# Another order of all 1610 words in a linear-attention and gated-MLP kernel's list

## The chip, the cores and the metric

The kernel runs on one core of a Trainium2 chip. The time is device microseconds of one execution; the comparisons rest on the median of several runs. The engines are PE (TensorE: matmuls, with PEld for loading weights), DVE (VectorE), ACT (ScalarE), POOL (GpSimd) and SP (SyncE), whose queue issues nearly all transfers.

## The reference

Gated linear attention with a state per head, then a gated MLP on its output, all in fp32:

```python
# q, k, v, alpha: (batch 4, heads 8, seq 768, head_dim 48)
for t in range(S):
    state = alpha[:, :, t, :, None] * state + einsum('bhd,bhe->bhde', k[:, :, t], v[:, :, t])
    y[:, :, t] = einsum('bhd,bhde->bhe', q[:, :, t], state)
x = y.transpose(0, 2, 1, 3).reshape(B * S, H * D)     # 3072 tokens x 384
g = x @ w_gate                                        # 384 x 1536
out = (g * sigmoid(g) * (x @ w_val)) @ w_out          # 1536 x 384
```

## The kernel before

The attention is cut into 16 units of 192 positions (four per batch), all 8 heads at once; a unit has three chunks of 64. The MLP is cut into 8 blocks of 384 tokens (two units each) times 12 slices of 128 of the inner width: 96 steps. Blocks 0 and 1 are done in two halves: steps 0 to 6 are the first seven slices of block 0, steps 7 to 13 those of block 1, 14 to 18 and 19 to 23 the rest; then come twelve steps for each further block. So g7 is the first product that needs block 1, that is, units 2 and 3, and g84 the first that needs block 7, units 14 and 15.

The weights come as 64-bit words. Each of the 20 groups of weights (two slices, the first three of one) is loaded raw, cut to fp32 in three steps, and split into a high part and a low part in fp32r. Products are the sum of three: high by high, high by low, low by high. So a g, a v and an o are nine matmuls of 384 columns each (three row blocks by three products).

All instructions are written down by one list, ORDER: 1610 words, each of the form engine:name@banks. The engine is t (PE), v (DVE), s (ACT), g (POOL) or y (SP); digits behind @ name the PSUM banks. The program goes through the list and writes each word's instructions to its engine's queue. Every engine works through its own queue in order, and waits at an instruction for whatever its operands need. There is no other scheduler. The words that matter here (u is a unit, c a chunk, n a group of weights, s a step):

- Lau, Lku, Lqu, Vu.i: loads of alpha, keys, queries, values. For units 0 to 3, pau, pku, pqu widen them (L405) and Tau, Tku, Tqu turn them on PE (L417), eau, eku, cqu copy them out; later units are transposed on DVE (tru, tku, tqu, L397).
- Gu, fu: the two scans of the decay on DVE (L461, L470); qu, mku: queries and keys scaled; qcu, vcu: copies of a part of the queries (L492) and of the values into U (L498).
- Su: scores (L552). mau.i: masked scores from PSUM to X on DVE (L586). Ku.c, kcu.c: keys turned on PE and copied out on ACT (L515, L516); kru.i is the same on DVE (L527).
- Buc or Bwu: the carry into the next chunks (L576); adu.c adds or copies it into the values or into SE (L599, L606, L608); deu carries SE into the next unit (L614).
- Yu: the unit's outputs (L630, L631, L647); yhu.i, ylu.i: their high and low part (L661 on ACT, L665 on DVE).
- Ru.kt, xu.kt: for units 0 and 1 the rows are brought into xT by PE; for all others xru.kt moves them from X to xT by transfers on SP (L701): ten for each unit. One xT serves a block.
- wln, wnv0 to wnv2, wna, wnp: load of a weight group (L298, L301), its cutting steps (L160, L161, L164), its high part (L341), its low part (L345).
- gs, sls, vs, hs, hhs, hls, os: gate product, SiLU (L724), value product (L716), h = SiLU times value (L728), its high part (L732) and low part (L737), output product (L748). g has one PSUM bank, called gps (bank 6), v one, called vps (bank 5): the next g waits for the SiLU of the one before, the next v for its h.
- otu.i, osu.i, plu.i: output rows copied, stored, and loaded again; wri, wci, Lcu, cku: loads and tests of the value ranges.

A transfer on SP waits for the one issued eight before it, besides what its operands need.

Of the kernel before, what the change touches and what calls it, by code (L numbers as in the profile page):

```python
# [48 lines left out]
y:La3 y:V1.1 y:V1.0 y:V1.3 y:V1.5 y:V1.2 v:de1 g:vc1 v:yl0.0 v:yl0.1 v:w3v2 s:pa2 t:S1@30 t:Bw1@2 s:qc1 s:pa3 v:ma1.0
v:ma1.1 y:wl4 s:w4v0 v:w4v1 s:ad1.0 v:ma1.2 v:w4v2 g:w4a g:w4p t:Ta2@65 s:ea2 v:G2 s:ad1.2 t:Y1@41 s:yh1.0 v:yl1.0  # L50
t:R0.1@6 t:R0.0@7 v:x0.0 s:x0.1 t:Ta3@35 t:R0.2@6 y:Lq2 s:pq2 t:Tq2@04 y:V2.4 y:V2.0 y:Lk2 s:pk2 y:V2.1 t:Tk2@27
s:yh1.1 v:yl1.1 t:R1.2@1 s:cq2 s:x0.2 s:x1.2 t:R1.0@0 s:x1.0 t:R1.1@4 s:x1.1 v:mk2 t:K2.0@7 y:wl10 t:K2.2@2 s:kc2.2
y:wl5 s:w5v0 t:g0 s:kc2.0 t:K2.1@1 s:kc2.1 y:V2.3 y:V3.3 y:V2.5 y:Lk3 g:pk3 t:Tk3@04 v:f2 v:q2 s:ea3 y:Lq3 s:pq3
g:lm0 g:qc2 s:sl0 s:w3a g:w3p y:V2.2 v:de2 s:vc2 t:S2@27 t:Bw2@1 s:ad2.0 s:ad2.2 t:g1 s:sl1 v:w5v1 t:v0 v:G3 v:f3
v:ma2.2 v:h0 v:ma2.0 y:wl6 t:Tq3@13 s:cq3 g:q3 v:w5v2 y:wl12 y:V3.1 v:mk3 s:hh0 y:V3.2 y:V3.0 v:ma2.1 y:V3.4 t:g2
g:qc3 g:lm1 s:w6v0 v:w6v1 y:wl8 s:w8v0 t:v1 v:h1 y:wl16 y:V3.5 v:de3 t:K3.0@1 s:kc3.0 s:w5a s:hh1 g:hl1 v:w6v2
t:S3@70 v:ma3.1 v:ma3.2 v:w5p y:wl9 y:wl7 t:K3.1@2 s:kc3.1 t:Y2@43 y:V4.5 s:yh2.0 v:yl2.0 s:yh2.1 v:yl2.1 v:ma3.0
y:wl11 y:V4.3 y:V4.0 y:La4 s:w6a g:w6p y:wl14 y:xr2.0 y:xr2.1 y:Lk4 y:xr2.2 t:Bw3@2 t:v2 s:sl2 v:h2 t:g3 t:v3 v:hl0
t:o0 t:o1 s:w9v0 v:w9v1 v:w9v2 s:vc3 s:w7v0 v:w7v1 s:ad3.0 v:w8v1 v:w7v2 s:w7a v:w8v2 v:w7p s:hh2 s:sl3 v:h3 g:hl2
s:w8a v:w8p t:K3.2@2 s:w9a v:w9p t:Y3@01 s:hh3 t:g4 s:yh3.0 s:yh3.1 v:yl3.1 v:yl3.0 y:xr3.2 y:V5.4 s:w11v0 v:w11v1  # L60
v:w11v2 s:sl4 t:v4 v:h4 s:w10v0 v:w10v1 v:w10v2 t:o2 g:hl3 s:w12v0 v:w12v1 s:hh4 v:hl4 s:kc3.2 s:w10a v:w10p v:tr4
t:o3 t:g5 s:sl5 t:v5 v:h5 s:w11a g:w11p v:w12v2 t:o4 y:wl13 s:w13v0 v:G4 s:hh5 g:hl5 t:g6 s:sl6 t:v6 v:h6 s:hh6 g:hl6
y:xr3.0 y:xr3.1 t:g7 s:sl7 t:v7 v:tk4 v:mk4 t:g8 y:V5.1 y:Lq4 y:V5.3 v:tq4 y:V5.5 y:V4.4 s:w12a y:V4.1 y:V5.2 t:o5
# [1038 lines left out]
```

## Time and profile before

| | us |
|---|---|
| median of 3 runs | 559.82 (559.21 to 559.98) |
| the profiled execution's own time | 563.47 |
| span of its trace | 561.8 |
| PE busy | 537.3 (96%) |
| DVE busy | 378.5 (67%) |
| ACT busy | 253.7 (45%) |
| POOL busy | 165.3 (29%) |

The span is the time from the first to the last instruction of the profiled execution; its own time holds 1.7 us more around it. The durations below are of that execution. Busy shares are averages over the whole span; a single place is read from the waits, the chain and the timelines.

### The profile page before, as it was taken

What the parts mean: (1) busy time and instruction counts of PE and PEld (TensorE: products, weight loads), DVE (VectorE), ACT (ScalarE), POOL (GpSimd) and SP (SyncE); (2) the same over time, 40 slices, a digit from 0 to 9 for tenths busy, and PEclk for the clock granted to TensorE, in tenths of its full rate; (3) what the DMA queues carried; (4) which work ended last, traced back from release to release, by engine and by line L of the source; (5) the groups of instructions that cost most, each with busy time, mean ns of one, the idle gap of its engine ahead of it and who ended that gap; (6) DMA issues with size and microseconds to landing.
All of it is one profiled execution on the core that took longest, in us unless ns stands there. A gap on an engine that the chain in (4) does not pass through costs nothing.

```text
span 561.8 us, 13698 instructions
## 1 busy us (share of the span) xinstructions
PE 537.3 (96%) x5510; PEld 524.7 (93%) x5510; DVE 378.5 (67%) x605; ACT 253.7 (45%) x570; POOL 165.3 (29%) x164
## 2 busy tenths in 40 slices
...
GB/s 254 198 224 312 193 158 127 220 132 68 126 161 132 139 125 179 195 118 85 146 159 86 163 66 155 170 32 125 109 145 29 72 80 119 98 123 119 148 121 115
...
## 3 DMA queue, kind: packets, MB, share of 16 engines
...
q8 instruction: 44, 0.72, 0.6%
...
## 4 chain that ended last, share of the span: by engine, by line
PE 88%; DVE 3%; DMA 3%; issue 1%; ACT 1%; SPq 1%; POOL 0%; DVEq 0%; ACTq 0%; POOLq 0%
PE g L716 26%; PE v L716 26%; PE ops L748 25%; PE A L576 3%; PE y L647 2%; PE s L552 2%; DMA xT<-X 1%; DMA raw<-in_moe_w_val_dram 1%; PE y L630 1%; PE y L631 1%; SPq L701 1%; DVE AT L470 1%; DMA Le<-in_alpha_dram 1%; DVE Gs L461 1%; DVE t L161 1%
## 5 line engine op out<-in xcount | busy, mean ns | idle before, releaser
L716 PE MATMUL g<-xT,w 128*128 128x384 f32 x864 | 167.9, 338 | 5.2 <-ACT h L724 3.5
L716 PE MATMUL v<-xT,w 128*128 128x384 f32 x864 | 167.6, 338 | 0.0
L748 PE MATMUL ops<-w,hh 128*128 128x384 f32 x576 | 157.5, 335 | 0.0
L716 PEld LDWEIGHTS g<-xT,w 128*128 128x128 f32 x864 | 150.8, 188 | 6.9 <-ACT h L724 3.8
L737 POOL TENSOR_TENSOR hl<-h,hh 128x384 fp32r<-128x384 f32 x65 | 69.4, 1069 | 297.8 <-ACT hh L732 277.3
L716 PEld LDWEIGHTS v<-xT,w 128*128 128x128 f32 x864 | 152.3, 189 | 0.4
L728 DVE TENSOR_TENSOR h<-h,v 128x384 f32<-128x384 f32 x96 | 53.1, 553 | 115.4 <-PE v L716 91.4
L748 PEld LDWEIGHTS ops<-w,hh 128*128 128x128 f32 x576 | 105.3, 188 | 0.9 <-DVE part L756 0.8
L732 ACT CAST hh<-h 128x384 fp32r<-128x384 f32 x96 | 49.1, 512 | 124.6 <-DVE h L728 90.0
L748 PE MATMUL ops<-w,hl 128*128 128x384 f32 x288 | 96.8, 336 | 0.0
L724 ACT ACTIVATE h<-g 128x384 f32<-128x384 f32 x96 | 46.9, 489 | 97.0 <-PE g L716 88.5
L527 DVE STREAM_TRANSPOSE K<-Gs 32x384 f32<-32x384 f32 x96 | 54.7, 570 | 2.4 <-PE A L576 0.5
L748 PEld LDWEIGHTS ops<-w,hl 128*128 128x128 f32 x288 | 54.0, 188 | 0.1
L486 POOL TENSOR_TENSOR X<-trq,AT 112x768 f32<-112x768 f32 x13 | 22.7, 1746 | 34.3 <-DMA xT<-X 10.4
L737 DVE TENSOR_TENSOR hl<-h,hh 128x384 fp32r<-128x384 f32 x31 | 17.5, 565 | 21.0 <-ACT hh L732 19.5
L345 POOL TENSOR_TENSOR w<-t,w 128x768 fp32r<-128x768 f32 (+1 forms) x14 | 25.5, 1825 | 19.8 <-ACT w L341 18.5
L470 DVE TENSOR_TENSOR_SCAN AT<-AT,back 128x771 f32<-128x771 f32 x16 | 30.4, 1899 | 0.6
L586 DVE TENSOR_TENSOR X<-s,mask 64x384 f32<-64x384 f32 (+1 forms) x48 | 26.4, 552 | 5.0 <-PE s L552 4.0
L461 DVE TENSOR_TENSOR_SCAN Gs<-AT,inj 128x772 f32<-128x772 f32 x16 | 28.0, 1752 | 0.6 <-ACT AT L794 0.5
L661 ACT CAST X<-y 112x384 fp32r<-112x384 f32 x28 | 12.3, 482 | 26.8 <-PE y L647 23.1
L318 ACT ACTIVATE wc<-wc,wbias 128x384 f32<-128x384 f32 x36 | 23.3, 647 | 1.2
L576 PE MATMUL A<-V,K 64*48 64x48 f32 (+1 forms) x720 | 22.1, 207 | 1.0 <-issue 0.9
...
## 6 DMA issues: line engine op xcount, KB each, us to landing
xT<-X SPq DMA_DIRECT2D x84, 72.0 KB, 2.2
...
```

Of the source, the lines that this page charges most:

```text
L345: eng.tensor_tensor(out=lo, in0=src, in1=hi.bitcast(F32), op=ALU.subtract)
L461: nc.vector.tensor_tensor_scan(*(x.rearrange("p g t -> p (g t)")[:, ::-1] for x in (Gs, AT, inj)), 0.0, op0=ALU.mult, op1=ALU.add)
L470: nc.vector.tensor_tensor_scan(Af, Af, back[:, 1 : n + 1], back[:, 0:1], op0=ALU.mult, op1=ALU.add)
L527: nc.vector.transpose(out=bass.AP(k0.tensor, k0.offset, [k0.ap[0], (G * 2 * D, NU), (2 * D, G), (1, 32)]), in_=Kg[j * BO + x : j * BO + x ...
L576: nc.tensor.matmul(to[j * BO : j * BO + D, g - gs.start, :], Ks[r, x, g, KC[j]], Vd[r, x, g, VC[j]], start=(x == 0 or not whole), stop=(x ...
L586: nc.vector.tensor_tensor(out=X[r, z, f * GF : (f + 1) * GF, :].rearrange("r g (c t) -> r g c t", c=NU), in0=sps[f][r].rearrange("r g (c t ...
L716: nc.tensor.matmul(pt, wsp[kind, f][a][:, kt * P : (kt + 1) * P], xT[blk][:, b_, kt, :], start=(n == 0), stop=(n == 3 * KT - 1),)
L724: nc.scalar.activation(h, acc.pop(("g", blk, f)), AF.Silu)
L728: nc.vector.tensor_tensor(out=h, in0=h, in1=acc.pop(("v", blk, f)), op=ALU.mult)
L732: nc.scalar.copy(out=hh, in_=acc["h", blk, f])
L737: eng.tensor_tensor(out=hl, in0=acc.pop(("h", blk, f)), in1=hh.bitcast(F32), op=ALU.subtract)
L748: nc.tensor.matmul(ops[blk][i], h[b_][:, i * P : (i + 1) * P], wsp["o", f][a], start=(first and n == 0), stop=(last and n == 2),)
```

## The change

Only the text of ORDER changes: the same 1610 words in another order. 84 of them go to another engine. The words of each engine are now 366 for PE (as before), 451 for DVE (443), 396 for ACT (387), 106 for POOL (123) and 291 for SP (as before). Most words of PE and DVE name other banks or stand at other places. The functions are untouched.

```diff
 ORDER = """
-y:La0 s:pa0 t:Ta0@23 s:ea0 y:wl0 v:w0v0 v:w0v1 y:Lk0 v:w0v2 g:w0a y:La1 s:pa1 g:w0p t:Ta1@53 y:Lq0 s:pq0 t:Tq0@71
+y:La0 y:wl0 s:pa0 t:Ta0@20 s:ea0 y:La1 s:pa1 y:Lq0 s:pq0 y:Lk1 y:Lk0 t:Ta1@67 s:pk0 v:w0v0 v:w0v1 v:w0v2 s:w0a g:w0p
...
```

Three places follow. First ACT (Activation) in unit 0, where the carried state SE, the values' copy U and the keys K are copied; before:

ACT before, from the last cutting step of w2 on:

```order
L160 ACTIVATE t2_353<-raw2_351,lbias_120 128x384
L606 COPY SE_109<-s0_0_240 48x96 x2
L606 COPY SE_109<-A2_0_296 48x96 x2
L515 COPY K0_105<-kps1_1_367 64x4x48
L516 COPY K0_105<-kps1_1_367 64x4x48
L599 COPY V0_77<-A2_0_296 48x8x48 x2
L515 COPY K0_105<-kps1_0_377 64x4x48
L516 COPY K0_105<-kps1_0_377 64x4x48
L515 COPY K0_105<-kps1_2_356 64x4x48
L516 COPY K0_105<-kps1_2_356 64x4x48
L341 CAST w1_386<-t1_199 128x384
```

The same place on ACT now:

```order
L794 COPY trq1_290<-pt1_2_1_286 128x128x3
L606 COPY SE_109<-s0_0_234 48x96 x2
L606 COPY SE_109<-A2_0_295 48x96 x2
L599 COPY V0_77<-A2_0_295 48x8x48 x2
L160 ACTIVATE t2_352<-raw2_350,lbias_120 128x384
L498 COPY U_101<-V0_77 64x3x96 x2
L515 COPY K0_105<-kps1_2_357 64x4x48
L516 COPY K0_105<-kps1_2_357 64x4x48
L515 COPY K0_105<-kps1_1_370 64x4x48
L516 COPY K0_105<-kps1_1_370 64x4x48
```

The copies of SE and of the state stand together and first; the copy of U, which POOL did, has come in behind them, and the cast of w1 has gone to POOL. In the whole list the masked scores of unit 0 (ma0.0 to ma0.2) stood ahead of the copies of SE (ad0.2) and now stand behind them.

Second, ACT around g7: raw13 is the load of weight group 13, h0_6 the SiLU of step 6 and h1_0 that of step 7. ACT before:

```order
L724 ACTIVATE h0_5_1279<-g0_5_1269 128x384
L341 CAST w11_1292<-t11_1215 128x768
L160 ACTIVATE t13_1308<-raw13_1305,lbias_120 128x768
L732 CAST hh0_5_1312<-h0_5_1279 128x384
L724 ACTIVATE h0_6_1326<-g0_6_1316 128x384
L732 CAST hh0_6_1339<-h0_6_1326 128x384
L724 ACTIVATE h1_0_1360<-g1_0_1350 128x384
```

ACT now:

```order
L732 CAST hh0_5_1302<-h0_5_1270 128x384
L341 CAST w11_1307<-t11_1256 128x768
L341 CAST w12_1310<-t12_1299 128x768
L724 ACTIVATE h0_6_1335<-g0_6_1315 128x384
L732 CAST hh0_6_1338<-h0_6_1335 128x384
L724 ACTIVATE h1_0_1370<-g1_0_1360 128x384
L515 COPY K0_105<-kps3_2_1138 64x4x48
L516 COPY K0_105<-kps3_2_1138 64x4x48
L160 ACTIVATE t13_1374<-raw13_1047,lbias_120 128x768
```

The first step of weight group 13 stood ahead of the SiLU of step 6 and stands behind that of step 7.

Third, SP at the end of the moves from X to xT for block 1 (X0 holds unit 2, X1 unit 3), SP before:

```order
L701 DMA xT1_1026<-X0_103 48x2x192 x2
L701 DMA xT1_1026<-X1_104 32x2x192
L701 DMA xT1_1026<-X1_104 48x2x192 x2
L435 DMA V1_78<-in_v_dram 64x4x48
L301 DMA raw13_1305<-in_moe_w_gate_dram 128x3x256
L301 DMA raw13_1305<-in_moe_w_val_dram 128x3x256
L701 DMA xT1_1026<-X1_104 48x2x192 x2
L701 DMA xT1_1026<-X1_104 32x2x192
L701 DMA xT1_1026<-X1_104 16x2x192
L701 DMA xT1_1026<-X1_104 48x2x192 x2
L701 DMA xT1_1026<-X1_104 16x2x192
```

SP now:

```order
L298 DMA raw14_1134<-in_moe_w_out_dram 128x768
L301 DMA raw14_1134<-in_moe_w_gate_dram 128x3x256
L701 DMA xT1_1039<-X1_104 16x2x192
L701 DMA xT1_1039<-X1_104 48x2x192 x2
L701 DMA xT1_1039<-X1_104 16x2x192
L701 DMA xT1_1039<-X1_104 48x2x192 x2
L701 DMA xT1_1039<-X1_104 32x2x192 x2
L701 DMA xT1_1039<-X1_104 48x2x192 x2
L701 DMA xT1_1039<-X0_103 32x2x192
L701 DMA xT1_1039<-X0_103 48x2x192 x2
L301 DMA raw16_1243<-in_moe_w_gate_dram 128x3x256
```

The loads among the moves of unit 3 have gone ahead of them (raw13 stands further up), and the last three moves of unit 2 have come behind them.

## Rows read from the trace of the kernel before

**Rows 1.** The page's first lines: span, busy time and share of each engine.

```profile
span 561.8 us, 13698 instructions
PE 537.3 (96%) x5510; PEld 524.7 (93%) x5510; DVE 378.5 (67%) x605; ACT 253.7 (45%) x570; POOL 165.3 (29%) x164
```

**Rows 2.** PE's waits over the span: waiter, releaser, us in total, times, longest.

```profile
PE g L716 <- ACT h L724: 3.5, 1, 3.5
PE y L647 <- POOL U L498: 2.7, 1, 2.7
```

**Rows 3.** The chain that ended last, in order of time: start us, us, what.

```profile
33.32 0.90 PE y L647 x32
...
47.25 1.56 PE v L716 x9
...
63.47 7.51 DMA xT<-X
...
77.21 5.97 DMA raw<-in_moe_w_val_dram
...
85.11 2.00 PE g L716 x9
87.11 2.88 PE v L716 x9
89.99 1.67 PE g L716 x9
...
215.02 1.34 issue
```

**Rows 4.** PE's timeline, 0 to 92 us: start us, us, engine, line, operation, tiles, count.

```profile
18.10 0.72 PE L576 MATMUL A<-V,K 128*48 128x48 f32 x24
...
24.91 0.90 PE L552 MATMUL s<-X,Gs 48*64 48x64 f32 x48
...
39.47 1.83 PE L716 MATMUL g<-xT,w 128*128 128x384 f32 x9
...
79.90 1.73 PE L716 MATMUL v<-xT,w 128*128 128x384 f32 x9
```

**Rows 5.** Two stretches: length, busy us and count per engine, PEclk, DMA share, GB/s.

```profile
30.00:35.00 5.00, 2.29 (x65) 1.96 (x61) 3.35 (x5) 2.15 (x8) 4.80 (x4) 1.00 0.82 275
...
87.00:88.00 1.00, 1.00 (x5) 1.00 (x4) 0.96 (x2) 0.80 (x2) 0.29 (x1) 0.50 0.83 151
```

**Rows 6.** ACT's timeline, 21 to 46 us; in brackets idle before and releaser.

```profile
21.03 0.48 ACT L606 COPY SE<-s 48x96 f32<-48x96 f32 x2 [2.25 <-DVE X L586]
...
22.05 0.31 ACT L515 COPY K<-kps 64x192 f32<-64x192 f32 x1
...
45.15 0.89 ACT L498 COPY U<-V 64x288 f32<-64x288 f32 x2
```

**Rows 7.** POOL's timeline, 29 to 41 us.

```profile
29.13 4.14 POOL L498 COPY U<-V 64x288 f32<-64x288 f32 x2
...
38.84 2.00 POOL L405 COPY wide<-L 128x576 f32<-128x576 f32 x1 [2.76 <-ACT xT L691]
```

**Rows 8.** DVE's timeline at the masks of unit 0 and the low parts of unit 3.

```profile
19.23 1.71 DVE L586 TENSOR_TENSOR X<-s,mask 128x384 f32<-128x384 f32 x3
...
69.08 1.02 DVE L665 TENSOR_TENSOR X<-y,X 112x384 fp32r<-112x384 f32 x2
```

**Rows 9.** Groups by line and shape, DVE and POOL: busy us, mean ns, idle before.

```profile
L737 DVE TENSOR_TENSOR hl<-h,hh 128x384 fp32r<-128x384 f32 x31 | 17.5, 565 | 21.0 <-ACT hh L732 19.5 <-issue 1.5
L345 DVE TENSOR_TENSOR w<-t,w 128x768 fp32r<-128x768 f32 x6 | 5.7, 955 | 0.2 <-ACT w L341 0.2
L486 DVE TENSOR_TENSOR X<-trq,AT 112x768 f32<-112x768 f32 x2 | 2.2, 1090 | 0.0
...
L345 POOL TENSOR_TENSOR w<-t,w 128x768 fp32r<-128x768 f32 x10 | 20.1, 2016 | 15.4 <-ACT w L341 14.2 <-POOL V L438 0.9
```

**Rows 10.** The page's part 6, DMA issues: count, KB each, median us to landing.

```profile
xT<-X SPq DMA_DIRECT2D x84, 72.0 KB, 2.2
```

**Rows 11.** SP's timeline, the last seven moves for block 1.

```profile
78.37 4.48 SPq L701 DMA_DIRECT2D xT<-X  x7
```

More of the change, by code (lines that the diff above doesn't have):

```diff
@@ L49 @@
[L49 to L63, printed above, removed]
@@ L129 @@
-s:hh77 y:os71.0 y:Lc10 v:ad15.0 v:ad15.1 y:Lc0 s:ck0 y:os71.2 t:g78 t:v78 t:o76 y:wr12 y:xr14.1 v:ma15.2 s:sl78 v:h78
-s:hh78 v:hl78 y:Lc5 s:ck5 t:g79 s:sl79 g:hl77 t:o77 t:o78 t:v79 v:h79 s:vc15 t:Y15@10 s:yh15.0 s:yh15.1 s:hh79 t:g80
-v:yl15.0 v:yl15.1 y:xr15.1 s:sl80 y:wr20 y:xr15.2 y:xr14.2 t:v80 s:wc12 v:h80 t:g81 v:hl79 t:v81 s:sl81 t:g82 t:o79
-s:hh80 v:hl80 t:o80 s:ck10 s:sl82 v:h81 t:v82 s:wc20 v:h82 t:g83 t:v83 s:hh81 g:hl81 t:o81 s:hh82 g:hl82 t:o82 s:sl83
-v:h83 s:hh83 v:hl83 t:o83 y:wr1 y:wr14 y:wr23 y:xr15.0 t:g84 s:wc14 v:ot83.0 y:os83.0 s:sl84 s:wc23 t:v84 v:h84
@@ L139 @@
[L139 to L141 removed]
+y:La0 y:wl0 s:pa0 t:Ta0@20 s:ea0 y:La1 s:pa1 y:Lq0 s:pq0 y:Lk1 y:Lk0 t:Ta1@67 s:pk0 v:w0v0 v:w0v1 v:w0v2 s:w0a g:w0p
+v:G0 t:Tq0@35 s:pk1 v:f0 v:q0 t:Tk0@12 v:mk0 y:wl1 s:w1v0 y:Lq1 v:w1v1 y:wl3 y:V0.3 s:ea1 v:G1 y:V0.1 y:V0.0 y:V0.2
@@ new lines @@
+t:Tk1@43 s:ek1 t:K0.1@5 s:kc0.1 t:S0@60 t:K0.0@3 s:kc0.0 v:w1v2 t:K0.2@1 s:kc0.2 s:w3v0 v:mk1 v:f1 g:pq1 t:Tq1@72
+s:cq1 y:V0.5 y:V0.4 t:Bw0@5 s:ad0.2 s:ad0.0 y:wl2 s:w2v0 y:V1.3 g:qc0 v:ma0.0 t:K1.2@4 y:wl4 s:vc0 y:V1.0 s:kc1.2
+t:K1.1@2 s:kc1.1 y:V1.4 y:V1.1 t:K1.0@3 s:kc1.0 v:ma0.1 v:ma0.2 t:Y0@70 y:V1.2 s:yh0.0 s:yh0.1 v:w3v1 v:w2v1 y:La2
+s:pa2 y:V1.5 g:w1a v:w1p s:w4v0 y:La3 s:pa3 g:q1 v:de1 t:S1@62 t:Bw1@3 s:ad1.0 v:w2v2 g:w2a y:Lq2 v:w3v2 v:yl0.0
+v:yl0.1 t:R0.1@7 g:qc1 v:ma1.0 v:ma1.1 v:w4v1 v:ma1.2 t:Ta2@05 s:ea2 v:G2 s:ad1.2 g:vc1 t:Y1@41 s:yh1.0 v:yl1.0
@@ new lines @@
+t:K3.1@4 s:kc3.1 y:wl9 v:f3 v:q3 t:S3@16 s:w6v0 t:K3.0@3 s:kc3.0 g:qc2 v:ma2.0 v:ma2.1 t:Y2@42 s:yh2.0 y:V3.4 y:wl8
+v:w5v2 s:w5a v:de3 t:Bw3@0 s:ad3.0 s:yh2.1 v:h1 s:hh1 v:w6v1 v:w6v2 v:yl2.0 v:ma3.2 g:qc3 v:ma3.0 v:yl2.1 y:wl12
+y:wl11 y:xr2.0 y:Lk4 y:wl13 y:xr2.1 s:w6a v:w6p t:v2 v:h2 v:ma3.1 t:o0 g:w5p t:g3 t:v3 v:w7v1 s:w9v0 s:hh2 v:hl2
+g:hl1 t:o1 t:o2 v:w7v2 s:w8v0 s:vc3 y:wl14 v:w8v1 t:K3.2@1 v:w9v1 v:w8v2 s:sl3 v:h3 s:w7a v:w7p v:w9v2 s:w8a v:w8p
+s:w10v0 v:w10v1 s:w9a v:w9p t:Y3@20 s:yh3.0 t:g4 s:sl4 s:hh3 g:hl3 s:yh3.1 v:yl3.1 t:v4 v:h4 v:yl3.0 y:xr3.1 y:xr3.0
@@ new lines @@
+y:xr3.2 y:xr2.2 y:wl16 t:g5 s:w11v0 v:w11v1 v:w10v2 t:v5 s:sl5 v:h5 s:hh4 v:hl4 v:w11v2 s:w10a v:w10p t:o3 t:o4
+s:w12v0 v:w12v1 s:hh5 v:hl5 v:w12v2 s:w11a v:w11p s:w12a g:w12p v:tk4 t:g6 t:v6 s:sl6 v:h6 s:hh6 g:hl6 v:tr4 v:G4
+y:V5.2 y:Lq4 y:V4.2 t:o5 t:g7 s:sl7 s:kc3.2 s:w13v0 t:v7 v:h7 t:o6 s:ot6.1 y:V4.4 y:os6.1 s:ot6.0 y:os6.0 y:La5 v:mk4
+v:w13v1 v:f4 s:w14v0 s:hh7 g:hl7 y:wl15 y:V5.0 y:V4.1 y:V4.0 y:wl17 t:g8 s:sl8 t:v8 v:h8 s:hh8 g:hl8 v:w14v1 t:g9
+s:w16v0 v:tq4 s:ot6.2 s:sl9 t:v9 v:h9 v:w13v2 t:o7 v:w14v2 s:w14a g:w14p v:q4 v:tr5 t:g10 t:v10 s:sl10 y:V5.4 s:w13a
@@ new lines @@
+s:sl16 s:ot13.2 s:hh15 g:hl15 v:w17v2 s:w17a g:w17p v:w18v2 s:w18a g:w18p t:v16 v:h16 v:ad4.2 y:La6 v:tr6 t:g17 t:v17
+s:sl17 v:h17 t:o14 t:o15 y:V5.1 y:Lk6 v:tk6 v:kr5.2 s:hh17 g:hl17 v:kr5.3 t:Y4@56 s:yh4.0 s:yh4.1 v:yl4.0 v:yl4.1
+y:V5.3 y:V5.5 v:G6 v:mk6 t:S5@10 t:B5@2 v:kr6.2 v:kr6.1 t:g18 s:sl18 t:v18 t:g19 s:hh16 g:hl16 t:o16 t:o17 y:Lq6
+y:os13.1 y:wl19 s:w19v0 v:w19v1 v:w19v2 s:w19a y:V6.0 y:os13.2 v:h18 v:f6 s:qc5 v:ma5.0 y:V6.4 y:V6.2 v:kr6.3 g:w19p
+s:sl19 t:v19 v:h19 y:V6.1 y:wr8 y:V6.5 y:pl18.2 s:hh18 g:hl18 v:tq6 s:hh19 g:hl19 t:g20 s:wc8 s:sl20 s:vc5 t:o18
@@ new lines @@
+v:h35 g:qc9 g:hl33 t:o33 t:o34 s:hh35 v:hl35 v:G10 v:f10 t:o35 v:ot35.2 s:ot35.1 y:os35.1 t:g36 t:v36 s:wc3 s:wc19
+v:ad8.1 v:ad8.2 t:Y8@41 s:sl36 v:h36 y:V9.0 y:V10.0 s:hh36 g:hl36 y:V9.4 y:wr15 y:V9.1 y:V10.1 v:ot35.0 y:Lq10
+v:kr9.3 s:yh8.0 s:yh8.1 v:yl8.0 v:kr9.2 t:g37 s:sl37 t:v37 v:h37 g:mk10 t:g38 s:sl38 t:v38 v:h38 v:yl8.1 t:g39 t:o36
+s:hh37 g:hl37 t:o37 t:v39 s:hh38 v:hl38 s:sl39 v:h39 s:hh39 g:hl39 t:g40 s:sl40 t:v40 y:V9.5 v:de9 s:vc9 y:V10.4
+t:g41 y:V10.2 y:xr8.0 y:xr8.2 y:xr8.1 v:tq10 g:q10 v:h40 s:sl41 v:kr9.1 t:S9@01 t:B9@2 s:qc10 v:tr11 t:o38 t:o39
@@ new lines @@
+v:ad10.2 s:sl46 t:v46 y:V11.1 v:h46 s:hh46 v:kr11.0 t:g47 s:sl47 y:os35.2 t:o45 g:hl46 t:o46 s:vc10 t:Y10@60 y:V11.2
+y:xr9.0 v:q11 v:tr12 t:S11@15 v:kr11.2 v:ma11.2 y:V11.3 y:V11.0 t:B11@2 s:yh10.0 s:yh10.1 v:yl10.0 y:Lk12 v:tk12
+y:wr7 t:v47 v:h47 v:de11 v:G12 g:mk12 s:hh47 v:hl47 t:g48 s:sl48 t:v48 v:h48 s:hh48 y:wr4 s:wc7 y:Lq12 y:V12.5
+y:os35.0 y:V12.2 g:hl48 t:g49 s:sl49 t:o47 s:ot47.0 y:La13 v:yl10.1 y:xr10.0 v:ot47.1 v:ad11.0 y:os47.1 y:wr11 s:wc26
+t:v49 v:h49 s:hh49 g:hl49 v:ad11.1 t:g50 t:v50 s:sl50 v:h50 s:ot47.2 t:g51 y:V12.1 t:o48 t:v51 s:sl51 v:h51 t:g52
@@ new lines @@
+t:o49 s:hh50 g:hl50 t:o50 v:tq12 s:hh51 g:hl51 v:f12 y:os47.0 y:xr10.2 y:xr10.1 y:wr9 s:wc11 t:v52 s:sl52 v:h52
+s:hh52 v:kr12.0 s:wc4 g:hl52 g:qc11 t:g53 s:sl53 t:v53 v:h53 v:q12 v:ma11.1 y:V12.3 y:V12.4 t:g54 y:Lk13 v:tr13
+y:Lq13 y:wr0 t:v54 s:sl54 v:h54 v:tk13 t:g55 t:o51 t:v55 t:o52 g:vc11 v:ma11.0 t:Y11@01 y:V13.2 v:kr12.3 v:G13 v:mk13
+s:hh54 y:wr28 v:kr12.2 g:hl54 s:sl55 v:h55 s:hh53 v:tq13 s:wc9 s:yh11.0 s:yh11.1 v:yl11.0 v:kr12.1 y:V12.0 y:V13.3
+v:yl11.1 y:os47.2 y:wr2 t:g56 g:hl53 t:o53 t:o54 s:sl56 s:hh55 s:wc0 g:hl55 y:La14 t:v56 v:h56 s:hh56 v:hl56 y:xr11.2
@@ new lines @@
+y:xr11.0 t:g57 s:sl57 v:f13 t:v57 s:qc12 t:S12@12 t:B12@0 s:ad12.0 y:xr11.1 g:q13 v:h57 v:ma12.1 v:kr13.3 v:ma12.0
+t:o55 t:o56 t:g58 y:V13.0 y:V13.5 s:hh57 g:hl57 y:wr5 y:Lk14 y:V13.1 v:kr13.0 v:ad12.1 v:ad12.2 v:ma12.2 t:v58 s:sl58
+v:h58 s:hh58 t:g59 t:o57 v:tr14 y:Lq14 v:kr13.1 g:hl58 v:G14 s:sl59 t:v59 v:h59 s:hh59 g:hl59 t:o58 v:tk14 y:La15
+g:mk14 v:f14 t:g60 t:v60 s:sl60 v:h60 s:hh60 t:g61 s:sl61 y:V13.4 t:v61 t:o59 v:hl60 v:h61 s:hh61 g:vc12 t:Y12@65
+y:V14.3 s:ot59.0 y:os59.0 g:vc13 s:wc5 s:yh12.0 s:wc2 s:yh12.1 v:kr13.2 v:yl12.0 v:de13 t:S13@12 t:B13@0 v:ad13.0
@@ new lines @@
+v:yl12.1 v:ad13.1 s:qc13 v:ad13.2 s:ot59.1 s:ot59.2 t:g62 s:sl62 s:wc28 t:o60 t:v62 v:h62 s:hh62 g:hl62 v:kr14.0
+t:g63 s:sl63 v:ma13.2 v:ma13.0 t:v63 v:h63 v:tq14 t:g64 t:v64 g:hl61 t:o61 t:o62 y:wr21 y:V14.4 y:V14.0 y:Lc5
+v:ma13.1 s:ck5 v:kr14.1 s:sl64 v:h64 t:Y13@51 y:V14.5 y:xr12.0 y:xr12.2 y:os59.2 y:os59.1 y:xr12.1 y:wr32 v:q14
+v:kr14.2 v:kr14.3 s:yh13.0 s:yh13.1 s:hh63 y:V14.1 y:V14.2 y:Lk15 s:hh64 g:hl63 t:S14@26 t:B14@0 v:ma14.2 v:yl13.0
+v:de14 v:ad14.0 v:tk15 t:g65 t:v65 t:o63 s:sl65 v:h65 s:hh65 g:hl65 s:wc32 t:g66 s:sl66 v:tr15 y:Lq15 v:yl13.1 t:v66
```

128 lines of the change are left out of this document (51 added, 77 removed).

## The prediction

> **What bounds the kernel now.** Read the share of busy time first, then TensorE's waits, then the chain of waits in order of time, then the engines' timelines at the places that the chain names. The profiled execution spans 561.8 us, and TensorE is busy for 537.3 of them [rows 1]. A word g, v or o of the MLP is nine matmuls and 1.56 us [rows 3]; there are 288 of them, 449 us, and no order makes them fewer. From 85.11 us until the last output product the chain of waits is TensorE and nothing else, but for five short pauses in which it waited for nothing that the profile shows, the longest 1.34 us [rows 3]. So an order can win in the first 85 us only, and can lose anywhere.
>
> In these 85 us the reader is to see two losses. The first is the way to the first product g0, which starts at 39.47 [rows 4]: the scores of unit 1 start at 24.91 [rows 4], the outputs of unit 1 wait 2.7 us for U on GpSimd [rows 2] and end at 34.22 [rows 3]. The second stands at g7, the first product of block 1. The product before it, v6, ends at 79.90 + 1.73 = 81.63 [rows 4]; g7 starts at 85.11 after 3.5 us of waiting for a SiLU [rows 2, 3], and then runs 2.00 us, v7 2.88 and g8 1.67 in place of 1.56 each [rows 3]. That is 1.87 us more, in a stretch where the granted clock is 0.50, the lower of TensorE's two levels [rows 5]. The place costs 3.48 + 1.87 = 5.35 us. Between g0 and g7 nothing is lost: 42.16 us passed, and the words there, counted at their durations in the chain, come to about 42.
>
> **The change part by part.** Every word stays; only places move, and 84 of the 1610 words change their engine.
>
> Unit 0. Before, ScalarE copies the first carried state (SE) at 21.03, after 2.25 us of idling for a mask product on VectorE [rows 6], which comes ahead of it in the old list. In the new list the copies stand ahead of the mask products, so they wait for TensorE's carry alone. The carry ended at 18.82 [rows 4] and nothing ahead of it is moved back, so the copies run at about 18.6 to 20.5. The mask products keep their place behind VectorE's chain of scans (19.23 to 20.9, rows 8), which I find unchanged: its inputs come as early as before. The copy of U for unit 0 goes from GpSimd to ScalarE (0.89 us, rows 6) and ends near 22.1, so Y0 ends near 22.9 instead of 24.9: 2.0 us won. ScalarE's six key copies of unit 1 (0.31 each, rows 6) follow to 24.0; S1 and its carry need the banks that these empty, and take about 2.5 us: 26.6.
>
> Unit 1. The copy of U on GpSimd took 4.14 us, of which the chain charges 2.7 to TensorE [rows 2, 7]. In the new list a cast of w2 and a copy of q, about 1 us each, stand ahead of it on GpSimd, behind VectorE's last step of w2 near 24.2; I put it at 26.0 to 30.1, with the slow duration of 4.14. Y1 can start when ScalarE has copied unit 1's state, near 28.3, and then ends near 31.0, for 34.22 before. Behind it the way to g0 was 39.47 - 34.22 = 5.25 us. It holds the repacking matmuls, two transposes and ScalarE's copies. A widening goes from ScalarE to GpSimd (2.00 us there, rows 7), and one copy from VectorE to ScalarE, so I give it 5.3 to 5.6. g0 starts near 36.3: 3.2 us won. The bounds are 0, if GpSimd and the copies take back what unit 0 gave, and 4.5, if U is copied in 0.9 us as on ScalarE.
>
> Weigh the slow copy once more: GpSimd's 4.14 us against 0.89 us for the same two copies on ScalarE [rows 6, 7]. The Trainium skill ("SBUF — State Buffer", section "Who interferes with whom") says that a VectorE instruction with two inputs from SBUF contends with a GpSimd instruction that reads SBUF, and that one of them is blocked outright. This speaks against the change, which gives VectorE more such subtractions beside GpSimd's copies. By the rule the copy stays at about 4 us, as I have taken it; without it the sum would be some 2 us lower.
>
> g7. Before, ScalarE's list has the first step of weight group 13 (raw13) ahead of the SiLU of step 6, and that load was issued at 77.21 and took 5.97 us [rows 3]. In the new list the load is issued ahead of unit 2's second move into xT, and its step stands behind the SiLU of g7. So the wait of 3.48 us goes, and with it the 1.87 us at the low clock: 5.35 us.
>
> What is late next at g7 is xT itself. It needs 20 moves from X to xT on the sync queue. The last group waits for VectorE's subtraction yl3.0; it ended at 70.10 before [rows 8]. In the new list 13 moves stand behind it with nothing between. Seven took 4.48 us to issue, 0.64 each [rows 11], and a move lands in 2.2 us [rows 10]: 13 x 0.64 + 2.2 = 10.5 us. VectorE's work from the scan of unit 1 to yl3.0 grows: the low parts of w1, w3, w4 and w6 come over from GpSimd (about 0.55 + 3 x 0.955), with one hl (0.565) and q3 (1.09); h4 (about 0.55) and a step of w10 (about 0.96) now stand ahead; one hl, one copy and the low part of w5 go (2.1). That is 4.5 us more [rows 9]. Of the old 50.9 us from 19.23 to 70.10, by the same counting, 43 were work and 8 were waits for TensorE. If the earlier TensorE work takes half of those waits away, yl3.0 ends near 70.9 and xT is complete near 81.4; if none goes, 74.6 and 85.1.
>
> TensorE itself is ready for g7 at 36.3 + 42.2 + 1.56, since the new list has o5 ahead of g7: 80.1. So the new wait is 1.3 us at best and 5.0 at worst. I take 2.1, nearer the best, since the same earlier start that frees VectorE's waits is what moves g0. Such a wait is shorter than the 2.71 us of unit 1, across which the granted clock stayed at 1.00 [rows 2, 5], so I add nothing for the clock.
>
> Later. Y4 and Y12 now use the banks of g and v, so the next g waits for their evacuation: S and B cover 1.8 us of the two casts and two subtractions, about 2.1. I add 0.6 for both together and for tight places that I don't see; bounds 0 and 3. VectorE's work between two h that are six steps apart, counted as above, exceeds TensorE's by 0.4 us at most, so I see no place where it must be late.
>
> Sum: -3.2 - 5.35 + 2.1 + 0.6 = -5.85 us. On the profiled execution's own time, 563.47, that gives 557.6; the median of the runs shown is 559.82, 3.65 lower, and there it gives 554.0.
>
> **The rivals.** *VectorE becomes the bound of the first 85 us.* For it: the 4.5 us more work, and low parts of weights on VectorE just ahead of the g and v that need them (that of w7 is due within 0.2 us of g4 by my count). Against it: the same subtraction takes 0.955 us there and 2.016 on GpSimd [rows 9], so the products get their weights sooner. All 8 us of waits stay, and xT is complete at 85.1; with 1.87 us at the low clock again, and one o more done than before, the gain is 1.56 + (85.11 - 85.1), about 1.6, and the time 558.2.
>
> *The order hardly does what it says:* what g0 wins is waited for again by loads. For it: the chip's transfers set the old stalls, one move took 7.51 us to land [rows 3] where 2.2 is usual [rows 10], and a list cannot shorten them. Against it: at g7 the load that was waited for is issued some 15 us earlier. Then g0 stays at 39.5, xT comes at 85 and the time is within 1 us of 559.8.
>
> *Slower, by the last block.* Before, 13 words (20.3 us) stand between the end of Y15 and g84; now 8 (12.5 us). On the sync queue 19 issues end with the moves for g84, two groups of unit 14 and a load among them. If those 19 start only when the last subtraction of unit 15 is done, 2.6 us after Y15 (two casts, two subtractions and an h, about 0.5 each), the last is issued 12.2 us later (0.64 each); at 7.51 us to land, as behind bulk loads [rows 3], g84 waits 2.6 + 12.2 + 7.5 - 12.5 = 9.8 us, and 1.87 more at the low clock. With -5.85 this gives +5.8, 565.6. It decides from 5.85 us on, that is, when the queue is held and the moves land late together. Against it: unit 14's moves need nothing of unit 15, and with them issued before, 10 x 0.64 + 2.2 + 2.6 = 11.2 us fit in 12.5. The Trainium skill ("DMA: Bandwidth & Descriptors", section "Queues, rings and completion order") has each DMA engine consume a queue's descriptors in ring order. The 7.51 us agree with that. By that rule the price stands wherever bulk is in front, and the chance hangs on the order alone.
>
> **How the numbers follow.** The forecast, 554.0, has 0.60; its own range is 551.5 to 556.5. VectorE as the bound has 0.17, no change 0.08, the last block or a like stall 0.12, and a gain beyond the forecast's range 0.03. The low end, 551.3, is -3.2 - 5.35 with no new wait, 8.55 below the median. The high end, 559.5, takes in the second case and stops short of no change; about 0.17 lies above it and 0.03 below. A difference of 0.2%, 1.1 us, is about what a measurement of this kernel can tell from none. Faster by more holds all of the forecast, the gain beyond it and nearly all of the second case: 0.79. Within: the third case, less its tails: 0.07. Slower: 0.14.
>
> **What would show it.** In the new trace: ScalarE's SE copies start before 19 us and wait for TensorE; Y1 ends near 31; g0 starts near 36.3; no SiLU wait at g7, but a wait there for a move into xT, under 3 us, and a granted clock of 1.00 through it; from g7 to the end a chain of TensorE alone. I am wrong if g0 starts after 38.5, if the clock falls to 0.50 at any place after 40 us, or if TensorE waits more than 2 us anywhere after g8.

## The result, and the profile after

The kernel after took 553.57 us, the median of 4 runs (552.74 to 554.53); the kernel before took 559.52 beside it (558.24 to 559.98). The ratio is 0.987, with a 95% interval of 0.983 to 0.991. The forecast was 554.0.

The page's first lines of the profiled execution (552.74 us), then TensorE's waits (waiter, releaser, us in total, times, longest), against [rows 1, 2]:

```profile
span 551.0 us, 13702 instructions
PE 536.4 (97%) x5510; PEld 523.7 (95%) x5510; DVE 384.8 (70%) x612; ACT 258.7 (47%) x581; POOL 136.5 (25%) x146
```

```profile
PE pt L417 <- POOL sel L369: 5.1, 1, 5.1
PE pt L417 <- ACT wide L405: 1.5, 2, 1.3
PE g L716 <- issue: 1.0, 1, 1.0
...
PE v L716 <- DVE h L728: 0.3, 1, 0.3
```

The two rows that I read in the kernel before, 3.5 us for a SiLU and 2.7 for U [rows 2], are both gone. What is left is the start (pt) and crumbs. Next TensorE's timeline at S1 and g0, ScalarE's at unit 0, and GpSimd's at unit 1 (start us, us, engine, line, operation, tiles, count; idle before in brackets):

```profile
23.20 0.92 PE L552 MATMUL s<-X,Gs 48*64 48x64 f32 x44 [0.29 <-ACT K L516]
...
34.47 1.85 PE L716 MATMUL g<-xT,w 128*128 128x384 f32 x9
```

```profile
18.24 0.50 ACT L606 COPY SE<-s 48x96 f32<-48x96 f32 x2
...
20.95 0.89 ACT L498 COPY U<-V 64x288 f32<-64x288 f32 x2
```

```profile
25.59 0.91 POOL L498 COPY U<-V 64x288 f32<-64x288 f32 x2
```

g0 starts at 34.47, for 39.47 [rows 4]. The copy of U that took 4.14 us [rows 7] takes 0.91. At g7 the chain of waits (start us, us, what), VectorE's yl3.1 and yl3.0, the sync queue's moves, and the clock (the number before the last two) are:

```profile
76.90 1.57 PE ops L748 x9
78.47 1.58 PE g L716 x9
80.05 1.56 PE v L716 x9
...
203.39 1.01 issue
```

```profile
67.26 0.56 DVE L665 TENSOR_TENSOR X<-y,X 112x384 fp32r<-112x384 f32 x1 [0.49 <-ACT X L661]
...
68.19 0.55 DVE L665 TENSOR_TENSOR X<-y,X 112x384 fp32r<-112x384 f32 x1
```

```profile
67.84 8.86 SPq L701 DMA_DIRECT2D xT<-X  x13
```

```profile
75.00:80.00 5.00, 5.00 (x30) 5.00 (x30) 5.00 (x5) 1.74 (x3) 2.70 (x2) 1.00 0.59 166
```

TensorE goes through o5, g7 and v7 without a gap, 1.56 to 1.58 us each, where before stood 3.48 us of waiting and a clock of 0.50 [rows 3, 5].

One thing did not fit. The two spans differ by 10.8 us, the medians by 5.95. The profiled run of before (563.47) lay above all its timed runs. So which of its two losses belongs to every run? The experiments ask that.

### The profile page after: what moved, and what is told of

It reads as the page before. It is cut to its first block, busy times and chain, and to the rows that moved or that the text cites. A ratio compares the mean times of both kernels' runs of the same rounds, so it can differ in the third digit from the quotient of the medians.

```text
span 551.0 us, 13702 instructions
## 1 busy us (share of the span) xinstructions
PE 536.4 (97%) x5510; PEld 523.7 (95%) x5510; DVE 384.8 (70%) x612; ACT 258.7 (47%) x581; POOL 136.5 (25%) x146
## 4 chain that ended last, share of the span: by engine, by line
PE 90%; DVE 3%; SPq 2%; ACT 2%; DMA 1%; issue 1%; DVEq 0%; ACTq 0%
PE g L716 26%; PE v L716 26%; PE ops L748 26%; PE A L576 3%; PE y L647 2%; PE s L552 2%; PE y L630 1%; SPq L701 1%; PE y L631 1%; DVE AT L470 1%; PE pt L417 1%; PE kps L511 1%; DMA Le<-in_alpha_dram 1%; DMA L<-in_k_dram 1%; DVE Gs L461 1%
## 5 line engine op out<-in xcount | busy, mean ns | idle before, releaser
L716 PE MATMUL g<-xT,w 128*128 128x384 f32 x864 | 167.5, 337 | 1.0 <-issue 1.0
L716 PE MATMUL v<-xT,w 128*128 128x384 f32 x864 | 166.9, 337 | 0.3 <-DVE h L728 0.3
L716 PEld LDWEIGHTS g<-xT,w 128*128 128x128 f32 x864 | 151.0, 188 | 2.2 <-issue 1.3
L716 PEld LDWEIGHTS v<-xT,w 128*128 128x128 f32 x864 | 150.9, 188 | 1.4 <-DVE h L728 0.9
L737 POOL TENSOR_TENSOR hl<-h,hh 128x384 fp32r<-128x384 f32 x63 | 67.7, 1076 | 308.1 <-ACT hh L732 294.1
L737 DVE TENSOR_TENSOR hl<-h,hh 128x384 fp32r<-128x384 f32 x33 | 18.8, 576 | 22.6 <-ACT hh L732 22.4
L470 DVE TENSOR_TENSOR_SCAN AT<-AT,back 128x771 f32<-128x771 f32 x16 | 32.5, 2031 | 0.6
L665 DVE TENSOR_TENSOR X<-y,X 112x384 fp32r<-112x384 f32 x28 | 15.2, 552 | 14.0 <-ACT X L661 13.8
L345 POOL TENSOR_TENSOR w<-t,w 128x768 fp32r<-128x768 f32 (+1 forms) x9 | 15.7, 1746 | 22.7 <-ACT w L341 17.8
```

Of the source, the lines that this page charges most:

```text
L470: nc.vector.tensor_tensor_scan(Af, Af, back[:, 1 : n + 1], back[:, 0:1], op0=ALU.mult, op1=ALU.add)
L716: nc.tensor.matmul(pt, wsp[kind, f][a][:, kt * P : (kt + 1) * P], xT[blk][:, b_, kt, :], start=(n == 0), stop=(n == 3 * KT - 1),)
L737: eng.tensor_tensor(out=hl, in0=acc.pop(("h", blk, f)), in1=hh.bitcast(F32), op=ALU.subtract)
```

## The experiments

Each kernel was timed in 5 rounds beside the kernel before, whose medians there were 561.3 to 562.3 (lowest 556.5, highest 565.2). The expectations were laid for 559.5, so I compare with the kernel before beside each run and not with their absolute times. A ratio is taken over the rounds and can differ by 0.3% from that of the two medians, so the times tell little of differences under 2 us. All edits are in the list of words alone. In x1, x2, x3 and x7 the list has four more lines, so L720 there is L716 here. To compare traces I use three stretches: up to g0, from g0 to g8, and the rest of the span. Where the new order has o5 and o6 ahead of g8, their 3.14 us are taken off g8 (8 rows like the chain's above give the starts).

| kernel | g0 | g0 to g8 | g8 to end | clock near 0.5 at |
|---|---|---|---|---|
| before | 39.47 | 50.5 | 471.8 | 87 to 90 |
| x1, before again | 39.43 | 45.9 | 471.6 | 24 to 30 |
| x6, unit 0 | 39.83 | 46.8 | 472.5 | 33 to 37 |
| x10, units 0 and 1 | 38.91 | 49.3 | 472.4 | 27 to 30, 85 to 88 |
| x2, load later | 38.46 | 46.6 | 471.9 | 25 to 28 |
| x12, units and load | 37.90 | 47.2 | 472.6 | nowhere |
| x3, new head | 35.68 | 50.3 | 473.6 | 178 to 180 |
| x7, new head, load later | 35.61 | 50.1 | 473.0 | 49 to 52 |
| after | 34.47 | 45.6 | 470.9 | nowhere |
| xa, after again | 37.48 | 45.6 | 471.8 | nowhere |
| x11, after, unit 0 old | 39.09 | 45.6 | 470.6 | 23 to 30 |

One place stands out in the last stretch: inside g24, the first product of block 2, x1 waits for a move into xT again, as x6 does (1.46 us) and x10 (0.79). After, xa and x11 don't wait there. TensorE's timeline of x1:

```profile
175.19 0.76 PE L720 MATMUL g<-xT,w 128*128 128x384 f32 x3 [1.21 <-DMA xT<-X]
```

**The kernel before again (x1).** No edit.

> The kernel before, word for word, a second time, to see whether its profiled run (563.47 us, 3.65 above the median of the timed runs of that time) was like the others. Theory T (the stall at step 7 is part of every run): 559.5 us within 0.8; the trace again has TensorE waiting 3 to 4 us for SiLU of step 7 behind the range check of weight load 13, that load landing near 84 us, and a granted clock near half in the 2 us after it. Rival R (the profiled run was out of the common at this place): the same 559.5, but the load lands some 3 us sooner, the wait is under 1.5 us and the clock stays at 1.00.

560.79 us, ratio 0.999 (0.997 to 1.002). The trace shows R at g7. The chain of waits, ScalarE's check of load 13, and the clock in the head:

```profile
79.04 2.81 DMA xT<-X
...
81.96 1.81 PE g L720 x9
```

```profile
79.99 0.99 ACT L164 ACTIVATE t<-raw,lbias 128x768 f32<-128x768 uint32 x1 [3.34 <-DMA raw<-in_moe_w_val_dram]
...
81.29 0.49 ACT L728 ACTIVATE h<-g 128x384 f32<-128x384 f32 x1
```

```profile
22.00:24.00 2.00, 0.87 (x12) 0.54 (x13) 1.69 (x4) 1.89 (x7) 0.00 (x0) 0.82 1.01 312
24.00:30.00 6.00, 6.00 (x167) 5.74 (x169) 2.00 (x3) 4.97 (x11) 3.90 (x5) 0.50 0.64 166
```

Load 13 is there at 79.99, not at 83.2; the SiLU ends at 81.78 and the last move into xT releases g7 at 81.96, after a wait of 0.37. So two things are late at g7 nearly together, and the load's landing varies by 3.3 us between two runs of one kernel (1.9 of them because it was issued later, at 77.21 for 75.29). Over the four traces with these words around g7 (before, x1, x6, x10) the stretch from g0 to g8 takes 50.5, 45.9, 46.8 and 49.3: 48.1 on the mean. The low clock that I read at g7 stands in the head instead, from 24 to 30, after TensorE was busy for only 0.87 of the 2 us before.

**The load alone (x2).**

```diff
-y:wl13 s:w13v0 v:G4 s:hh5 g:hl5 t:g6 s:sl6 ... t:g7 s:sl7
+y:wl13 v:G4 s:hh5 g:hl5 t:g6 s:sl6 ... t:g7 s:sl7 s:w13v0
```

> The kernel before with one word moved: the range check of weight load 13 on ScalarE stands behind SiLU of step 7 instead of ahead of steps 6 and 7. T (the profile's 3.48 wait and 1.87 of low clock belong to every run): 5.35 us less, 554.2 us. R (they don't): 1 to 2 us less, 557.5 to 558.5 us. A third reading, that the wait only moves to the next thing that is late (the moves of xT or the weights of load 13 themselves): within 0.8 of 559.5.

559.57 us, 0.9964 (0.9938 to 0.9989): 2.0 us less. That is R's size, not T's 5.35. But the trace shows the third reading: the wait moves to the next thing that is late, a move of xT. TensorE's timeline:

```profile
81.70 1.80 PE L720 MATMUL g<-xT,w 128*128 128x384 f32 x9 [1.04 <-DMA xT<-X]
```

From g0 to g8 this trace takes 46.6, no less than x1's 45.9 with the load's check at its old place.

**The new head in the old list (x3), and with the load later (x7).**

```diff
-all words as before has them
+the words of after up to t:g2, then those left, in the order of before
```

> The order of after as far as the gate product of step 2, then all other words as before has them (so the range check of load 13 still stands ahead of SiLU of step 7). The theory of two places: the first gate product starts 4 to 5 us sooner (39.47 to about 34.5) and the gain stays: 554.5 to 556 us. Rival A (the whole gain is at step 7; a sooner start only makes TensorE wait longer there, since the load's landing doesn't move with it): within 1 us of 559.5.

> Both: the head of after as far as step 2, and the range check of load 13 behind SiLU of step 7. If the two places add up and each has the size that the profiles show (5.0 and 5.35): 549 to 550 us, under the kernel after. If they add up and the stall at step 7 is small in usual runs: 553 to 554 us, as after. If they are one gain (the sooner head is lost again at step 7 unless the check moves): x3 near 559.5, x2 near 558, and this one 553 to 555.

x3: 561.03 us, 0.9975 (0.9947 to 1.0003). x7: 559.92 us, 0.9981 (0.9957 to 1.0005). g0 comes 3.8 us sooner, and nothing of it is left at g7, which starts at 82.55 in x3 and 81.79 in x7, for 81.96 in x1. x3 has rival A's number; x7 missed all three of its readings. Three rows of x3's chain, and TensorE's timeline in x7:

```profile
50.47 1.70 POOL X L490
...
80.80 1.75 DMA xT<-X
82.55 1.83 PE g L720 x9
```

```profile
48.63 1.38 PE L421 MATMUL pt<-ident,wide 128*128 128x128 f32 x6 [2.08 <-ACT SE L610]
49.66 3.01 PE L720 MATMUL v<-xT,w 128*128 128x384 f32 x9
```

Most of it is lost at the seam, where the new words end and the old ones go on. TensorE waits 2.08 us there for ScalarE's copies of SE, in x3 as in x7; then in x3 q3 on GpSimd is late for unit 3 (0.68 us), and in x7 the clock is at 0.50 from 49 to 52, so that one v takes 3.01 us. At g7 itself the moves cost 1.22 us in x3 and about 0.8 in x7. So these two runs don't show by themselves that the moves hold back a sooner head. The queue's own times speak for it: in the eight traces with the old list from step 2 to g8, g0 lies between 35.6 and 39.8, and g7 never starts before 81.7. The sync queue issues almost without a rest from 56 us to the last move, its last seven moves for block 1 begin between 75.1 and 78.4, and the move that g7 waits for lands at 81.7 to 82.8 in the chains of x1, x2, x3 and x7. What stays in place is the moves, where rival A named the load.

**Unit 0 alone (x6), both units (x10), and with the load later (x12)**, all in the kernel before.

```diff
-t:Bw0@0 v:ma0.2 g:qc0 ... g:vc0 ... t:K1.2@1 s:ad0.2 ... s:ad0.0 t:K1.0@6
+t:Bw0@0 s:ad0.2 s:ad0.0 v:ma0.2 g:qc0 ... s:vc0 ... t:K1.2@1 ... t:K1.0@6
-g:w2a g:w2p ... g:vc1          (x10 and x12, added to the lines above)
+g:vc1 g:w2a g:w2p
```

> The kernel before with three words of unit 0 changed and nothing else: the SE copies (two words) on ScalarE right behind the carry products, ahead of the second weight checks, and the copy of U on ScalarE instead of GpSimd. By the step as I forecast it (it brings Y of unit 0 forward, and with it all of the head): 2 to 3.2 us less than before. Rival (Y of unit 0 comes sooner, but Y of unit 1 still waits for its own U on GpSimd and VectorE's masks, so the first gate product moves by under 0.7 us): within 1 us of before.

> The kernel before with unit 0 as in the last comparison (SE copies and U on ScalarE) and, added to that, U of unit 1 on GpSimd ahead of the two weight splits that stood before it. Theory (both U copies must be out of the way): U of unit 1 ends before 28 instead of 32.3, Y of unit 1 starts when SE of unit 1 is there, at 30.5, and the first gate product near 37.5: 1.5 to 2.5 us less than before. Rival (the splits that now come later hold the first gate product): within 1 us of before.

> The kernel before with the edit of units 0 and 1 and with the range check of load 13 behind SiLU of step 7. If the two places add: the gain of x10 and the 2.0 us of the later load, 556.5 to 558 us. If the sooner head is lost at the moves of xT for step 7, whose time the queue of issues sets (in the four kernels with the moves as before, the last of them landed between 81.7 and 82.8 whatever the head did): no better than the later load alone, 559 to 560.

x6: 561.44 us, 1.0006 (0.998 to 1.003). x10: 561.38, 0.998 (0.996 to 1.001). x12: 559.61, 0.998 (0.995 to 1.001). x6 is its rival: S1, right behind Y0, comes 2.4 us sooner (22.50 for 24.91), but U of unit 1 on GpSimd ends only 1.0 sooner, and the clock of 0.50 behind it takes the rest. x10 is within its rival's 1 us, but its interval takes in the theory too. x12 has its rival's number; beside the kernel before it is 2.7 us less by the medians and 1.2 by the ratio, so the times do not exclude that the two edits add. GpSimd's and VectorE's timelines of x6, and the clock there:

```profile
27.95 4.33 POOL L498 COPY U<-V 64x288 f32<-64x288 f32 x2
```

```profile
28.11 0.94 DVE L161 SCALAR_TENSOR_TENSOR t<-raw,t 128x768 uint32<-128x768 uint32 x1
28.97 0.54 DVE L586 TENSOR_TENSOR X<-s,mask 128x384 f32<-128x384 f32 x1
29.44 0.94 DVE L164 SCALAR_TENSOR_TENSOR t<-raw,t 128x768 uint32<-128x768 uint32 x1
30.31 1.75 DVE L461 TENSOR_TENSOR_SCAN Gs<-AT,inj 128x772 f32<-128x772 f32 x1
```

```profile
33.00:36.00 3.00, 3.00 (x25) 2.78 (x14) 1.12 (x2) 1.53 (x3) 2.01 (x2) 0.51 0.41 77
```

In x10 and x12 the same copy takes 1.91. No split holds up TensorE in x10, as its rival had it: two pauses that wait for nothing that the profile shows (1.29 and 0.70 us) and the clock of 0.50 from 27 to 30 stand ahead of its g0. There g7 still waits, in x10 for the SiLU and with TensorE at the lower of its two levels behind it (0.50, 1.2 GHz), in x12 for the moves:

```profile
83.31 2.01 PE L716 MATMUL g<-xT,w 128*128 128x384 f32 x9 [2.10 <-ACT h L724]
```

```profile
85.00:86.00 1.00, 1.00 (x4) 1.00 (x4) 0.97 (x2) 0.58 (x2) 0.49 (x1) 0.50 0.97 263
```

```profile
PE g L716 <- DMA xT<-X: 2.8, 2, 1.7
```

Against x1, x12's head won 1.5 us and its stretch from g0 to g8 gave 1.3 back: g7 starts at 81.73 for 81.96, and in x2 at 81.70. In the traces the two local edits do not add.

**After again (xa), and after with one part undone (x11, x5).**

> The kernel after, word for word, beside the same runs of before as the three below. All theories: a ratio of 0.985 to 0.991. What it is for: whether after scatters like before (whose timed runs in the last comparison lay between 556.5 and 564.4), and a second trace of after. If the scatter of before comes from the stalls at step 7, after stays within 3 us from lowest to highest and its first 20 us of TensorE work again lose 6 to 7 us.

554.79 us, 0.991 (0.987 to 0.994); 553.13 to 558.93, so after scatters too, and the expected 3 us were too few. Its head loses 3.0 us more than in the first trace (g0 at 37.48), where I had expected the same; 1.65 of it stand in one pause inside the products of the carry that waits for nothing that the profile shows, and 0.83 in a second, inside the products of Y1. From g0 to g8 it is the first trace again; behind g8 it takes 0.8 us more. The 13 moves begin 3.0 us later than in after, just as g0 does. The sync queue:

```profile
70.84 8.80 SPq L701 DMA_DIRECT2D xT<-X  x13
```

```diff
-t:Bw0@5 s:ad0.2 s:ad0.0 ... g:qc0 v:ma0.0 t:K1.2@4 ... s:vc0 ... v:ma0.1 v:ma0.2 t:Y0@70
+t:Bw0@5 v:ma0.2 g:qc0 v:ma0.0 v:ma0.1 g:vc0 ... t:K1.2@4 s:ad0.2 ... s:ad0.0 t:K1.0@3 ... t:Y0@70
```

> The kernel after with the other part undone: between the carry products and Y of unit 0 the words stand as before has them (all masks ahead of the SE copies, these behind the weight check, U of unit 0 on GpSimd); nothing else. Theory: SE ends near 22.5 instead of 20.3 and all that follows in the head is 2 to 2.5 us later, lost time in the first 20 us of TensorE work 8.5 to 10 instead of 6.2 to 9.3, 2 us more than after. Rival (unit 0 alone decides nothing, as in the kernel before with unit 0 changed): within 0.8 us of after.

557.11 us, 0.991 (0.988 to 0.994). The trace shows the mechanism: SE waits for the masks again and ends at 21.9, and the clock falls. ScalarE's timeline and the windows:

```profile
20.87 0.49 ACT L606 COPY SE<-s 48x96 f32<-48x96 f32 x2 [1.95 <-DVE X L586]
```

```profile
24.00:30.00 6.00, 6.00 (x183) 5.74 (x181) 1.76 (x3) 3.59 (x8) 2.46 (x4) 0.54 0.19 49
```

g0 is at 39.09, 1.6 later than in xa and 4.6 later than in after. The 13 moves follow it again:

```profile
72.46 9.43 SPq L701 DMA_DIRECT2D xT<-X  x13
```

So with g0 nearly as late as in before, the new list keeps its 45.6 us from g0 to g8. But the times can't tell the size: the ratio is that of xa, and 0.4% above that of after, within the intervals.

```diff
-y:Lk4 y:wl13 y:xr2.1 ... t:o3 t:o4 s:w12v0 v:w12v1 s:hh5 ... t:g7 s:sl7 s:kc3.2 s:w13v0
+y:Lk4 y:xr2.1 ... t:o3 t:o4 y:wl13 s:w12v0 v:w12v1 s:w13v0 s:hh5 ... t:g7 s:sl7 s:kc3.2
```

> The kernel after with one part undone: weight load 13 is issued as late as before has it (behind the first products of step 4 and the 13 moves of xT) and its range check stands ahead of SiLU of steps 6 and 7 again; nothing else. Theory S (the stall at step 7 is real, of 0.7 to 5.4 us by the traces so far, 2.6 on the mean of three): 2 to 5 us more than after, TensorE waiting for SiLU of step 6 or 7. Rival (the stall cost next to nothing and the gain was all ahead of it): within 1 us of after. Against before: S gives a ratio of 0.994 to 0.999, the rival 0.989 to 0.992.

569.13 us, 1.014 (1.011 to 1.017): some 14 us more than after by the ratios, nearly three times the most that S expected. The sync queue, ScalarE, TensorE and the clock:

```profile
69.89 8.92 SPq L701 DMA_DIRECT2D xT<-X  x13
78.91 0.54 SPq L301 DMA_DIRECT2D raw<-in_moe_w_gate_dram  x1
...
80.57 0.49 SPq L301 DMA_DIRECT2D raw<-in_moe_w_val_dram  x1
```

```profile
86.68 0.98 ACT L160 ACTIVATE t<-raw,lbias 128x768 f32<-128x768 uint32 x1 [12.39 <-DMA raw<-in_moe_w_val_dram]
```

```profile
88.84 0.69 PE L748 MATMUL ops<-w,hh 128*128 128x384 f32 x1 [9.90 <-ACT w L341]
```

```profile
81.00:90.00 9.00, 1.01 (x2) 0.50 (x2) 1.91 (x3) 2.56 (x4) 0.00 (x0) 0.51 0.50 167
```

The load now stands behind the 13 moves and lands at 86.6, later than in before (83.2, ahead of the last seven moves), and all that ScalarE has behind its check waits. The load and its check were moved together; in the new list their places together are worth more than the whole gain.

**Two crosses at step 6 (x8, x9).**

```diff
-one list
+x8: the words of after up to t:g6, then those left, in the order of before
+x9: the words of before up to t:g6, then those left, in the order of after
```

> The order of after as far as the gate product of step 6, then all other words as before has them. Theory H (the gain is TensorE's time in the head: 11.1 us lost beside the work up to the first steps in the second trace of before, 6.2 in after, and the head must be kept until units 2 and 3 are through): 5 to 6.5 us less than before, ratio 0.988 to 0.991. Rival A (what counts is the queue of moves and loads around step 7, whichever order the rest has): as here that queue is also new up to step 6, the same. Rival L (the gain is spread over the 90 later steps): within 1.5 us of before.

> The order of before as far as the gate product of step 6, then all other words as after has them; the range check of load 13 stands ahead of SiLU of step 6, as before. H: as before, within 1.5 us. L: 4 to 6 us less than before. If it comes out between (2 to 3 us less), the later order has a part.

x8: 563.34 us, 1.005 (1.002 to 1.008). x9: 564.55 us, 1.006 (1.003 to 1.009). Both are slower than both parents, which no theory had. TensorE's waits in x8 show new ones at and behind the seam, for the SiLU and for h; the 2.5 us for nothing shown (issue) stand in g30, where other traces pause too:

```profile
PE v L716 <- DVE h L728: 2.5, 3, 1.3
PE g L716 <- issue: 2.5, 1, 2.5
PE g L716 <- ACT h L724: 2.2, 2, 1.7
```

Its head is the new one (g0 at 35.31), as that of x9 is the old one (39.58). So a list cut in two says nothing of the parts: its cost is in the seam. In x9 the profiled run took 4.9 us more than its span, where the others took 1.7; what fills that the profile doesn't show.

## Why the prediction was right, step by step

The time was right, and so was most of the place, the first 85 us. But the sizes rested on one trace, and the runs correct them. Means of the table: the old list needs 39.5 to g0 (before and x1), 48.1 to g8 (four traces) and 472.1 behind it (the same four); the new one 36.0, 45.6 and 471.4 (after and xa). That is 3.5 + 2.5 + 0.7 = 6.7 us, for 5.95 measured beside it and 6.5 in the second comparison. The 0.7 lies behind g8, where I had said that no order can win: the old list waits for moves at g24 (1.21 us in x1), and in the trace that I read only 0.4 us stood there, for nothing that the profile shows.

- *g0 3.2 us sooner:* 5.0 in the first trace and 2.0 in the second. The SE copies ran at 18.24 for 18.6, and U of unit 0 ended at 21.84 for 22.1, as worked out. U of unit 1 was mis-sized: I kept 4.14 us as its duration, and it took 0.91 in both traces of after. It isn't slow by itself; it waits out VectorE's instructions with two inputs from SBUF that run beside it, as far as the durations show. In x6 these are 0.94 + 0.94 + 1.75 us, and with 0.91 they make 4.54, for 4.33 measured; in x10 one of 0.95 makes 1.86, for 1.91; in after only a mask product is beside it, whose input s is in PSUM, and nothing is added. The rule of the Trainium skill that I weighed ("SBUF — State Buffer", section "Who interferes with whom") says that such an instruction contends with a GpSimd instruction that reads SBUF, and the traces agree with it. My error was to look at how much VectorE does and not at what runs in those microseconds. And my upper bound of 4.5 us for a short copy was too low by 0.5.
- *5.35 us at g7:* the mechanism was half of it, and the size was that of one run. The load's check does hold up the SiLU (x1, x5), but without it the moves hold up g7 (x2). My own rows had that: the last moves were issued near 82 [rows 11] and landed near 84 by the 2.2 us of [rows 10], an estimate, so over 2 of the 3.48 us would have stayed with the load out of the way. From g0 to g8 this run lost 2.4 more than the mean of the four, and the load alone gave 2.0.
- *A new wait of 2.1 us for the moves:* none. I had all 13 moves wait for yl3.0. It ended at 68.74 for 70.9, about as much sooner as g0, but the queue had begun the moves at 67.84, when yl3.1 ended (67.82); the last lands as TensorE arrives. In after, xa and x11 the moves begin 33.4 us behind g0 (67.84, 70.84 and 72.46), and from g0 to g8 the three take 45.6 to 0.03 us, whenever g0 comes. So the new list hands on a sooner head whole, and the old one does not. In the old list the moves were the second cause of the wait at g7, hidden behind the first; I named them for the new one alone.
- *0.6 us later:* the rest was 0.7 shorter (g24). The rivals of the last block and of VectorE did not come; no h was late by more than 0.3.
- *The clock:* I argued that a wait under 2.71 us leaves it at 1.00. In x10 it fell to 0.50 after one of 2.10 at g7. In before it stayed at 1.00 in the head; in x1, the same words, it was 0.50 from 24 to 30.

So the errors of 5.35 (too large) and of 2.1 (not there) had opposite signs and nearly cancelled, and that is luck. What the runs show is that a sooner head gains only where the moves follow it: in the old list the head alone gave 0 to 1.5 us (x3, x6, x10), the later load alone 2, and in x12 the moves took back what the head had won. That the new order of the queue needs the sooner head is not shown, and x11 speaks against it: g0 at 39.09, and still 0.991. The queue's new order alone, in the old list, was not tried. How much of the gain is unit 0's in the new list stays open (x11).
